# Groups 2 to 7 of layer one's first matrix as seven products of half blocks, with block sums taken from the decode and weight places from a list

## The chip, the cores and the metric

The kernel runs on one core of a Trainium2 chip. The metric is the device time of one execution in microseconds, from runs on the chip. The engines are TensorE (PE; its weight loads are PEld), VectorE (DVE), ScalarE (ACT), GpSimd (POOL) and SyncE (SP), whose queue issues most of the DMA transfers.

## What is computed

An attention with a local window and block summaries, and behind it two layers of two matrices each. x has 1536 tokens of 512 features.

```python
def _moe_ref(x, w_in, w_out):            # layer one: w_in 512x2048, w_out 2048x512
    h = x @ w_in
    g = h * (1.0 / (1.0 + np.exp(-1.702 * h)))
    return (g @ w_out).astype(np.float32)

def _moe2_ref(x, w_gate, w_val, w_out):  # layer two: 512x1536 twice, 1536x512
    gate = 1.0 / (1.0 + np.exp(-(x @ w_gate)))
    val = x @ w_val
    return (gate * val @ w_out).astype(np.float32)

def reference(**kwargs):
    attn_out = _attn_ref(q, k, v)        # 2 batches, 8 heads, 768 tokens, 64 features
    x = attn_out.transpose(0, 2, 1, 3).reshape(1536, 512)
    return _moe2_ref(_moe_ref(x, w_in, w_out), w_gate, w_val, w_out2)
```

## The kernel before

Each factor of a product is held as a high and a low part (H and L), each of a type that TensorE takes in one pass, and a product is three matmuls: low times high, high times low, high times high. Tokens go in three blocks of 512 (`TB`), the 512 features in four chunks of 128 (`KC`), split into `LO` and `HI`. The hidden features go in groups of 256, two halves of 128 each: eight groups in layer one (`n1`), six in layer two (`n2`). A weight comes from memory as 64-bit words into a `raw` buffer (two of them, `fetch`, line 157) and is decoded on DVE and ACT (`decode`, line 91) into a high and a low tile. `load` (line 168) is a generator that stands between other work; `pull` (line 446) takes its next step and `need` (line 451) takes steps until a weight is there.

The weight tiles, 128x1024 each, lie in three rings: `w_a` with 8 places, `w_b` with 4 and `w_c` with 2 (lines 85 and 747). In layer two `w_a` holds the first two matrices, `w_b` the block sums and `w_c` the last matrix.

Layer one works in steps of a group and a token block (line 133). `first` (line 368) makes two projections of 12 matmuls into two PSUM banks (`ps_h`), the sigmoid on ACT, and in `gate_by` (line 358) the product on DVE, the high part on ACT and the low part on POOL. `second` (line 395) makes four steps of 6 matmuls into the banks `ps_o`, and DVE adds each to `acc`. Four (group, block) steps, groups 0 and 1 for blocks 0 and 1, run between the units of the attention (`EARLY`, `filler`); the others follow in a plain loop (line 758) in which `second` of a step runs behind `first` of the next one. There `ps_o` has six banks.

Layer two takes blocks 0 and 1 together. `token_sums` (line 239) makes four combinations of their halves, `combine` (line 200) makes four combinations of the quarters of a weight, for which it first adds high and low part again (line 205), and `pair` (line 262) makes seven products per matrix of 6 matmuls each (`product`, line 117) where the plain form has eight. ACT copies product 1 into a second PSUM bank, onto which products 6, 7 and 4 add, and DVE adds held products to others (`total`, line 289). `single` (line 323) does block 2 in the plain way. In layer two the products take the six banks and `second` the two (line 778), and the steps of `second` stand between products.

Of the program, SP's order is written out by hand; the other engines' orders are worked out at build time from the order of the text and an estimate of each instruction's time, so that an instruction that is ready can be put ahead of an earlier one that isn't.

Of the kernel before, what the change touches and what calls it, by code (L numbers as in the profile page):

```python
# [28 lines left out]
def attention_moe_moe2_kernel(ctx: ExitStack, tc: tile.TileContext, ins: dict, out: bass.AP):  # L29
# [54 lines left out]
    w_slots, sg_slots, gh_slots, gl_slots = (Slots(t) for t in ("w", "sg", "gh", "gl"))  # L84
    w_a = pool([w_slots], 8, "w_a")
    pool([gh_slots, gl_slots], GF, "g_a")
    pool([sg_slots], 2, "sg_a")
    acc_a = ctx.enter_context(tc.tile_pool(name="acc_a", bufs=1))
    ps_h = ctx.enter_context(tc.tile_pool(name="ps_h", bufs=2, space=PSUM))

    def decode(raw, hi_out, lo_out):

        n = raw.shape[1] // 2
# [9 lines left out]
        ts(out=b, in0=tail, scalar1=29, scalar2=None, op0=ALU.logical_shift_right)  # L105
        yield
# [3 lines left out]
        nc.scalar.copy(hi_out, af)  # L110
        yield
        nc.vector.tensor_tensor(out=lo_out, in0=af, in1=hi_out, op=ALU.subtract)
# [19 lines left out]
    groups = [(1, g) for g in range(n1)] + [(2, g) for g in range(n2)]  # L132
    steps = [(1, g, blk) for blk in range(NTB) for g in range(2)]
    steps += [(1, g, blk) for g in range(2, n1 - 2) for blk in range(NTB)]
    steps += [(1, g, blk) for g in (n1 - 2, n1 - 1) for blk in range(2)] + [(1, g, 2) for g in (n1 - 2, n1 - 1)]
# [11 lines left out]
    pieces, weights, raws, ready = [], {}, [], {}  # L147
# [20 lines left out]
    def load(slots, layer, g, i):  # L168
        raw, shape = raws.pop(0)
        hi, lo = (slots.tile(list(shape), F32R, name=f"w{layer}_{g}_{i}{x}") for x in "HL")  # L170
        parts = decode(raw, hi.rearrange("p a n -> p (a n)"), lo.rearrange("p a n -> p (a n)"))
        for step, _ in enumerate(parts):
            if step == 1 and (layer, g) != (1, 0):
                fetch()
            yield
        return hi, lo

    def load_group(layer, g):
        tiles = weights[layer, g] = []
        ready[layer, g] = 0  # L180
        for i in range(len(mats[layer])):
            tiles += yield from load(w_slots, layer, g, i)
            ready[layer, g] += 1
            yield

    class Ring:


        def __init__(self, pool):
            self.pool = pool  # L190

        def tile(self, shape, dtype, name):
            return self.pool.tile(shape, dtype, tag="w", name=name)

# [5 lines left out]
    def combine(g, i):  # L200

        hi, lo = weights[2, g, i]
        flat = "p a n -> p (a n)"
        w, s = (wtmp.tile([P, KC, GF * P], F32, tag=t, name=f"{n}{g}_{i}") for t, n in (("da", "wf"), ("db", "ws")))
        nc.vector.tensor_tensor(out=w.rearrange(flat), in0=hi.rearrange(flat), in1=lo.rearrange(flat), op=ALU.add)  # L205
        yield
        s = s.rearrange("p a (k f) -> p a k f", f=P)
        for n, a, b, op in (
            (0, block(w, 1, 0), block(w, 1, 1), ALU.add),
            (1, s[:, 0], block(w, 0, 0), ALU.subtract),  # L210
            (2, block(w, 0, 0), block(w, 1, 0), ALU.subtract),
            (3, block(w, 0, 1), s[:, 1], ALU.subtract),
        ):
            nc.vector.tensor_tensor(out=s[:, n], in0=a, in1=b, op=op)  # L214
            if n % 2:
                yield
# [3 lines left out]
        nc.vector.tensor_tensor(out=sl.rearrange(flat), in0=s.rearrange(flat), in1=sh.rearrange(flat), op=ALU.subtract)  # L220
        sums[g, i] = sh, sl
        yield

    sums = {}

    def prepare():
# [219 lines left out]
    def pull(n):  # L446
        for _ in range(n):
            if next(coming, True):
                break
# [401 lines left out]
```

## Time and profile before

| | us |
|---|---|
| median of 3 runs | 630.01 (629.63 to 630.9) |
| the profiled execution | 629.99 |
| its span, first to last instruction | 628.1 |
| mean granted clock of TensorE | 0.997 of full |

The attention, with the early steps of layer one, takes the first 124 us, layer one the time to about 340, layer two the rest. "Busy" counts time in which an engine executes; matmuls overlap on PE, so its busy share alone doesn't say that it has no room. The chain of waits is followed back from the last instruction, at each step to what released it.

### The profile page before, as it was taken

The numbers are of one execution on the slowest core, as the hardware profiler recorded it, in microseconds if no ns is written. First come the engines' busy times: TensorE is split into PE (matmuls) and PEld (weight loads), VectorE is DVE, ScalarE is ACT, GpSimd is POOL, SyncE is SP. The second block draws the span as 40 slices with busy tenths as digits, with TensorE's granted clock in tenths as the row PEclk, the third lists the DMA queues.
The fourth block names the chain that finished last, engine by engine and source line by source line (L and its number), as shares of the span: only waits on it lengthen the run. The fifth ranks groups of instructions, "written<-read, shape, count | busy, mean of one in ns | idle before, by whom it ended". The sixth has DMA issues, their size and how long they took to land.

```text
span 628.1 us, 8342 instructions
## 1 busy us (share of the span) xinstructions
PE 613.1 (98%) x3162; PEld 499.9 (80%) x3162; DVE 430.8 (69%) x628; ACT 282.5 (45%) x560; POOL 194.8 (31%) x164
## 2 busy tenths in 40 slices
PE   7898999999999999999999999999999999999997
PEld 4676787778888888888888887888887888888886
DVE  6699666488976665565379995279499479496524
ACT  4688657546443334232246645444344244333310
POOL 6797676233132313132222030120031120130210
PEclk9899999999999999999999999999999999999999
DMA  9997752044521222100001304012113012100004
GB/s 311 347 328 254 242 126 64 2 134 141 176 86 67 68 67 68 67 2 1 0 13 61 129 0 135 0 68 78 57 67 118 17 67 74 61 1 0 2 33 168
DMA packets 25160, 58.08 MB, mean 92 GB/s; under 512 B 1568, under 2 KB 1824, under 8 KB 25120
## 3 DMA queue, kind: packets, MB, share of 16 engines
q1 hardware_dynamic: 24400, 56.24, 27.6%
q10 hardware_dynamic: 720, 1.31, 0.6%
q8 instruction: 25, 0.41, 0.3%
q14 instruction: 15, 0.12, 0.1%
HBM read 53.08 MB, written 3.15 MB: 90 GB/s over the span
## 4 chain that ended last, share of the span: by engine, by line
PE 86%; DVE 9%; ACT 2%; issue 1%; DMA 1%; SPq 0%; DVEq 0%; ACTq 0%
PE ps_o L349 35%; PE ps_h L349 20%; PE ps_v L124 8%; PE ps_y L124 7%; PE ps_x L124 5%; PE ps_h L124 4%; PE ps_s L559 3%; PE ps_x L611 2%; PE ps_p L592 1%; DVE wf L205 1%; DVE ws L214 1%; DMA vt<-in_vt 1%; ACT e L572 1%; DVE nm L564 1%; DVE sg L364 1%
## 5 line engine op out<-in xcount | busy, mean ns | idle before, releaser
L366 POOL TENSOR_TENSOR gl<-sg,gh 128x512 fp32r<-128x512 f32 x84 | 119.5, 1424 | 393.7 <-ACT gh L365 372.0
L429 DVE TENSOR_TENSOR acc<-ps_o,acc 128x512 f32<-128x512 f32 x143 | 97.2, 686 | 56.9 <-PE ps_o L349 56.8
L365 ACT CAST gh<-sg 128x512 fp32r<-128x512 f32 x84 | 52.0, 620 | 89.8 <-DVE sg L364 79.6
L349 PE MATMUL ps_o<-gh,w_1L 128*128 128x512 f32 x192 | 74.5, 395 | 1.6 <-ACT gh L365 1.5
L349 PE MATMUL ps_h<-xH,w_0L 128*128 128x512 f32 x192 | 75.2, 396 | 0.5 <-DVE acc L429 0.5
L349 PE MATMUL ps_o<-gl,w_1H 128*128 128x512 f32 x192 | 75.4, 393 | 0.0
L349 PE MATMUL ps_h<-xL,w_0H 128*128 128x512 f32 x192 | 75.0, 391 | 0.0
L349 PE MATMUL ps_o<-gh,w_1H 128*128 128x512 f32 x192 | 74.8, 390 | 0.0
L349 PE MATMUL ps_h<-xH,w_0H 128*128 128x512 f32 x192 | 74.8, 390 | 0.0
L364 DVE TENSOR_TENSOR sg<-ps_h,sg 128x512 f32<-128x512 f32 x48 | 32.9, 687 | 44.1 <-ACT sg L373 43.8
L349 PE MATMUL ps_o<-w_2H,gl 128*128 128x512 f32 (+1 forms) x146 | 56.2, 388 | 1.0 <-ACT acc L425 0.6
L349 PE MATMUL ps_o<-w_2H,gh 128*128 128x512 f32 (+1 forms) x146 | 56.4, 386 | 0.0
L349 PE MATMUL ps_o<-w_2L,gh 128*128 128x512 f32 (+1 forms) x146 | 56.4, 386 | 0.0
L373 ACT ACTIVATE sg<-ps_h 128x512 f32<-128x512 f32 x48 | 28.3, 595 | 61.2 <-PE ps_h L349 61.2
L107 DVE SCALAR_TENSOR_TENSOR da<-da,db 128x1024 uint32<-128x1024 uint32 x34 | 43.9, 1290 | 14.4 <-ACT da L103 14.0
L103 ACT ACTIVATE da<-da 128x1024 f32<-128x1024 f32 x34 | 36.1, 1061 | 30.6 <-DVE da L102 28.6
L349 PEld LDWEIGHTS ps_o<-gh,w_1L 128*128 128x128 f32 x192 | 35.9, 188 | 9.3 <-ACT gh L365 2.0
L349 PEld LDWEIGHTS ps_h<-xH,w_0L 128*128 128x128 f32 x192 | 36.0, 188 | 8.2 <-DVE acc L429 0.9
L349 PEld LDWEIGHTS ps_h<-xH,w_0H 128*128 128x128 f32 x192 | 36.0, 188 | 7.6
L349 PEld LDWEIGHTS ps_o<-gh,w_1H 128*128 128x128 f32 x192 | 36.1, 188 | 7.3
L349 PEld LDWEIGHTS ps_o<-gl,w_1H 128*128 128x128 f32 x192 | 36.1, 188 | 7.3 <-POOL gl L366 0.2
L349 PEld LDWEIGHTS ps_h<-xL,w_0H 128*128 128x128 f32 x192 | 36.0, 188 | 7.4
(162 smaller groups left out, 1244.5 us busy)
## 6 DMA issues: line engine op xcount, KB each, us to landing
raw<-in_moe_w_out SPq DMA_DIRECT2D x13, 1024.0 KB, 4.9
raw<-in_moe_w_in SPq DMA_DIRECT2D x8, 1024.0 KB, 7.3
raw<-in_moe_w_gate SPq DMA_DIRECT2D x6, 1024.0 KB, 5.1
raw<-in_moe_w_val SPq DMA_DIRECT2D x6, 1024.0 KB, 5.1
q<-in_q SPq DMA_DIRECT2D x20, 256.0 KB, 7.5
vwin<-in_v SPq DMA_DIRECT2D x6, 768.0 KB, 8.1
k<-in_k SPq DMA_DIRECT2D x8, 400.0 KB, 6.5
out<-acc SPq DMA_DIRECT2D x11, 256.0 KB, 2.0
```

Source lines behind the costliest of these rows:

```text
L103: nc.scalar.activation(af, af, AF.Prelu, scale=REBIAS, alpha=-2.0 ** 32)
L107: nc.vector.scalar_tensor_tensor(out=a, in0=a, scalar=3, in1=b, op0=ALU.logical_shift_left, op1=ALU.bitwise_or)
L124: nc.tensor.matmul(ps, lhsT=a[x][:, kk, :], rhs=b[y][:, kk, :], start=start and i == 0, stop=i == n - 1, skip_group_check=True,)
L205: nc.vector.tensor_tensor(out=w.rearrange(flat), in0=hi.rearrange(flat), in1=lo.rearrange(flat), op=ALU.add)
L349: nc.tensor.matmul(ps, lhsT=a, rhs=b, start=i == 0, stop=i == n - 1)
L364: nc.vector.tensor_tensor(out=sg, in0=val, in1=sg, op=ALU.mult)
L365: nc.scalar.copy(gh, sg)
L366: nc.gpsimd.tensor_tensor(out=gl, in0=sg, in1=gh, op=ALU.subtract)
L373: nc.scalar.activation(sg, ps, AF.Sigmoid, scale=1.702 if layer == 1 else 1.0)
L429: nc.vector.tensor_tensor(out=a[:, m, :], in0=ps, in1=a[:, m, :], op=ALU.add)
L559: nc.tensor.matmul(ps[:, j, :], lhsT=t[:, j, :], rhs=kt[:, j, :], start=False, stop=j == G - 1)
L611: nc.tensor.matmul(ps[64 * e:64 * e + 64, j, :], lhsT=x[:, h * D:(h + 1) * D], rhs=y[:, j, 64 * e:64 * e + 64], start=n == 0, stop=n == le ...
```

## The change

Layer one's groups 2 to 7 now take `pair` and `single`, as layer two does. For them the combinations of blocks 0 and 1 of the attention's output are made by `input_sums` in twelve steps, eight of them between the last units of the attention. A weight's block sums are made in `load`, straight from the decoded value, with no addition of high and low part, in layer two as well; `combine` is gone. Layer one's order of products is 1, 5, 2, 6, 3, 7, 4, and steps of `second` stand behind products as the lists in the last hunk say: in a pair those of block 2 of the group before, beside the single products those of blocks 1 and 0 of the same group, two behind each. From group 2 on `second` has two PSUM banks and the products six. Group 6's block 2 is done after group 7's pair, so that blocks 0 and 1 end before block 2. Weight places are no longer rings: `w_free` is a list of 14 places (8 and 6), `take` takes the one that was freed first and `drop` gives a weight's places back. A decode whose places are not free waits in the text, not on the engine.

```diff
+    def places(n, name):
+        p = ctx.enter_context(tc.tile_pool(name=name, bufs=1, reuse_waits="tile"))
+        w_free.extend((p, f"{name}{i}") for i in range(n))
+    def take(shape, name, key):
+        p, tag = w_free.pop(0)
+        w_held.setdefault(key, []).append((p, tag))
+        return p.tile(shape, F32R, tag=tag, name=name)
+    def drop(*key):
+        w_free.extend(w_held.pop(key))
+    places(8, "w_a")
...
+    def load(layer, g, i, early):
...
+        if (layer, g, i) == (1, 1, 1):
+            scratch.append(wraw.tile([P, KC, TB], F32, tag="raw", name="scratch"))
+        elif not early:
+            fetch()
         yield
...
+        while len(w_free) < 2:
+            yield
+        hi, lo = (take(list(shape), f"w{layer}_{g}_{i}{x}", (layer, g, i)) for x in "HL")
...
+        if layer == 1 and (g < 2 or i == 1) or layer == 2 and i == 2:
+            return
+        w = af.rearrange("p (a n) -> p a n", n=shape[2])
+        s = wtmp.tile([P, 4, KC // 2, P], F32, tag="db", name=f"ws{layer}_{g}_{i}")
+        for n, x, y, op in (
+            (0, block(w, 1, 0), block(w, 1, 1), ALU.add),
+            (1, s[:, 0], block(w, 0, 0), ALU.subtract),
+            (2, block(w, 0, 0), block(w, 1, 0), ALU.subtract),
+            (3, block(w, 0, 1), s[:, 1], ALU.subtract),
+        ):
+            nc.vector.tensor_tensor(out=s[:, n], in0=x, in1=y, op=op)
+            if n == 1:
+                yield
+        while len(w_free) < 2:
+            yield
...
+        nc.scalar.copy(sh.rearrange(flat), s.rearrange(flat))
+        yield
+        nc.vector.tensor_tensor(out=sl.rearrange(flat), in0=s.rearrange(flat), in1=sh.rearrange(flat), op=ALU.subtract)
...
-    def combine(g, i):
...
+    def input_sums():
+        tt = nc.vector.tensor_tensor
+        f1, f3 = scratch[0][:, LO], scratch[0][:, HI]
+        f2 = t_a.tile([P, KC // 2, TB], F32, name="f2")
+        h1, l1, h3, l3 = (t_tile(x) for x in ("1H", "1L", "3H", "3L"))
+        def whole(to, blk, half):
+            tt(out=to, in0=xH[blk][:, half], in1=xL[blk][:, half], op=ALU.add)
+        whole(f1, 0, LO)
+        yield
+        whole(f3, 1, LO)
+        yield
+        tt(out=f1, in0=f3, in1=f1, op=ALU.subtract)
+        yield
+        whole(f2, 1, HI)
+        yield
+        tt(out=f3, in0=f2, in1=f3, op=ALU.subtract)
+        nc.scalar.copy(h3, f3)
+        yield
...
+        tt(out=l2, in0=f2, in1=h2, op=ALU.subtract)
+        fetch()
...
         def out(i, to, x, own=None):
+            if layer == 1:
+                gate = sg_slots.tile([P, TB], F32, "sg")
+                nc.scalar.activation(gate, x, AF.Sigmoid, scale=1.702)
+                gate_by((1, g, *to), x, gate)
+                return
...
-        for n in "1256734":
-            for i in range(2):
+        for n in ("1526374", "1256734")[layer - 1]:
+            for i in range(layer):
...
+            if t >= 4 * HP + LD:
+                next(folding)
...
+        places(6, "w_b")
...
+        def run(main, rest=iter(()), after=()):
+            for n, _ in enumerate(main):
                 pull(1)
                 next(folding, None)
+                for _ in range(after.count(n)):
+                    next(rest, None)
+            for _ in rest:
+                pull(1)
+                next(folding, None)
...
+        for g in range(2):
+            run(first(1, g, 2))
+            drop(1, g, 0)
+            if g == 0:
+                run(second(1, 0, 2, False))
+                drop(1, 0, 1)
         ps_f, ps_o, o_tag = ps_o, ps_h, "h"
+        top = n1 - 1
+        for g in range(2, n1):
+            need((1, g, 0), (1, g, 0, "s"))
+            for _ in folding if g == 2 else ():
+                pass
+            if g < top:
+                run(pair(1, g), second(1, g - 1, 2, False), (0, 2, 4, 5))
+                drop(1, g - 1, 1)
+            else:
+                run(pair(1, g), seconds(1, g - 1, 1, 0), range(7))
+            drop(1, g, 0, "s")
+            need((1, g, 1))
+            if g != top - 1:
+                n = min(g, top - 1)
+                run(single(1, n), seconds(1, g, 1, 0), (0, 0, 1, 1, 2, 2, 3, 3))
+                drop(1, n, 0)
+        folding = token_sums()
+        run(single(1, top), second(1, top - 1, 2, False), range(4))
```

## Rows read from the trace of the kernel before

**Rows 1.** The page: engine totals (busy us, share, instructions), and granted clock in 40 slices.

```profile
PE 613.1 (98%) x3162; PEld 499.9 (80%) x3162; DVE 430.8 (69%) x628; ACT 282.5 (45%) x560; POOL 194.8 (31%) x164
...
PEclk9899999999999999999999999999999999999999
```

**Rows 2.** The chain of waits in order of time: start us, us, what.

```profile
64.10 0.69 PE ps_x L611 x16
...
160.62 5.44 PE ps_o L349 x24
...
367.27 2.21 DVE wf L205
...
476.30 2.72 PE ps_x L124 x12
```

**Rows 3.** Busy time by stretches: us, then engines (x instructions), clock, DMA share, GB/s.

```profile
160.00:320.00 160.00, 160.00 (x707) 132.55 (x706) 100.44 (x138) 55.80 (x81) 42.15 (x30) 1.00 0.17 53
400.00:600.00 200.00, 199.72 (x882) 164.96 (x881) 141.97 (x187) 78.46 (x113) 38.34 (x27) 1.00 0.14 48
```

**Rows 4.** What PE waited for, 64 us to the end: us, times, longest.

```profile
PE ps_o L349 <- ACT acc L425: 0.6, 1, 0.6
PE ps_x L611 <- DVE pt L597: 0.6, 1, 0.6
PE ps_h L349 <- DVE acc L429: 0.5, 1, 0.5
PE ps_o L349 <- DVE acc L429: 0.3, 1, 0.3
```

**Rows 5.** Busy time by stretches, the two slices in which PE's count falls.

```profile
360.00:380.00 20.00, 19.58 (x87) 15.89 (x85) 19.76 (x27) 9.74 (x14) 5.46 (x4) 1.00 0.08 18
...
460.00:480.00 20.00, 19.72 (x88) 16.00 (x87) 19.06 (x24) 7.78 (x12) 6.73 (x5) 1.00 0.10 31
```

**Rows 6.** Groups on DVE: line, shapes, count | busy us, mean ns | idle before, releaser.

```profile
L107 DVE SCALAR_TENSOR_TENSOR da<-da,db 128x1024 uint32<-128x1024 uint32 x34 | 43.9, 1290 | 14.4 <-ACT da L103 14.0
...
L112 DVE TENSOR_TENSOR w_0L<-da,w_0H 128x1024 fp32r<-128x1024 f32 x14 | 18.5, 1325 | 1.5 <-ACT w_0H L110 1.5
...
L220 DVE TENSOR_TENSOR sL<-ws,sH 128x1024 fp32r<-128x1024 f32 x12 | 14.6, 1216 | 2.0 <-ACT sH L219 2.0
L214 DVE TENSOR_TENSOR ws<-wf 128x256 f32<-128x256 f32 x24 | 10.5, 479 | 0.2
L205 DVE TENSOR_TENSOR wf<-w_1H,w_1L 128x1024 f32<-128x1024 f32 x6 | 10.5, 1743 | 0.2
...
L205 DVE TENSOR_TENSOR wf<-w_0H,w_0L 128x1024 f32<-128x1024 f32 x6 | 9.2, 1541 | 0.1
L290 DVE TENSOR_TENSOR sg<-ps_y,sg 128x512 f32<-128x512 f32 x12 | 8.2, 687 | 8.7 <-PE ps_y L124 8.7
...
L249 DVE TENSOR_TENSOR acc<-acc,acc 128x1024 f32<-128x1024 f32 x3 | 3.6, 1208 | 0.0
```

**Rows 7.** Groups on POOL and ACT, columns as in rows 6.

```profile
L366 POOL TENSOR_TENSOR gl<-sg,gh 128x512 fp32r<-128x512 f32 x84 | 119.5, 1424 | 393.7 <-ACT gh L365 372.0
...
L373 ACT ACTIVATE sg<-ps_h 128x512 f32<-128x512 f32 x48 | 28.3, 595 | 61.2 <-PE ps_h L349 61.2
...
L219 ACT CAST sH<-ws 128x1024 fp32r<-128x1024 f32 x12 | 12.7, 1055 | 11.6 <-DVE ws L214 8.5 <-PE ps_o L349 2.9 <-PE ps_h L349 0.2
```

**Rows 8.** Busy time by stretches, a slice at the end of the attention.

```profile
100.00:120.00 20.00, 19.98 (x169) 15.65 (x168) 9.97 (x24) 14.41 (x48) 9.54 (x9) 1.00 0.01 1
```

**Rows 9.** The chain of waits where the attention has ended.

```profile
125.76 1.23 DVE w_0L L112
127.64 8.50 PE ps_h L349 x36
```

**Rows 10.** The timeline at the end: start us, us, engine, operation, [idle before, releaser].

```profile
623.26 0.69 DVE L429 TENSOR_TENSOR acc<-ps_o,acc 128x512 f32<-128x512 f32 x1 [0.67 <-PE ps_o L349]
...
624.01 0.19 PEld L349 LDWEIGHTS ps_o<-w_2H,gl 128*128 128x128 f32 x1 [0.28 <-DVE acc L429]
```

More of the change, by code (lines that the diff above doesn't have):

```diff
@@ L131, in attention_moe_moe2_kernel @@
     n2 = w_gate.shape[1] // (GF * P)
[L132 to L135, printed above, removed]
+    steps = [(1, g, blk) for blk in range(2) for g in range(2)]
     ends = {1: n1 - 1, 2: n2 - 1}
@@ L166, in fetch @@
             raws.append((raw, (P, n, m // 2)))
[L168 to L184, printed above, removed]
@@ L224, in attention_moe_moe2_kernel, with t_tile @@
[L224 to L237 removed]
+    def t_tile(name):
+        return (t_b if name[0] == "2" else t_a).tile([P, KC // 2, TB], F32R, tag=f"t{name}", name=f"t{name}")
@@ L260, in attention_moe_moe2_kernel, with pair @@
     tsum = {}
-    def pair(g):
+    def pair(layer, g):
         def sums_of(n, i):
-            return tuple(x[:, n] for x in sums[g, i])
+            return tuple(x[:, n] for x in weights[layer, g, i, "s"])
         def a(i, r, c):
-            return tuple(block(x, r, c) for x in weights[2, g, i])
+            return tuple(block(x, r, c) for x in weights[layer, g, i])
         b11, b21, b22 = ((xH[n][:, h], xL[n][:, h]) for n, h in ((0, LO), (0, HI), (1, HI)))
@@ L321, in pair, with single @@
                 yield
-    def single(g):
+    def single(layer, g):
         for f in range(GF):
             sg = None
-            for i in range(2):
-                wh, wl = weights[2, g, i]
+            for i in range(layer):
+                wh, wl = weights[layer, g, i]
                 ps = ps_f.tile([P, TB], F32, tag="o", name="ps_h" if i == 0 else "ps_v")
@@ L443, in attention_moe_moe2_kernel, with need @@
     EARLY_UNITS = 10
-    coming = (x for n in range(2) for x in load_group(*groups[n]))
+    order = [(1, g, i) for g in range(n1) for i in range(2)] + [(2, 0, 0), (2, 0, 1)]
+    for g in range(n2):
+        order += [(2, h, i) for h, i in ((g + 1, 0), (g, 2), (g + 1, 1)) if h < n2]
+    coming = (x for n, key in enumerate(order) for x in load(*key, n < 2))
     def pull(n):
         for _ in range(n):
-            if next(coming, True):
-                break
-    def need(layer, g, n):
-        while ready.get((layer, g), 0) < n:
-            pull(1)
+            next(coming, None)
+    def need(*keys):
+        for key in keys:
+            tries = 0
+            while key not in weights:
+                pull(1)
+                tries += 1
+                assert tries < 100, (key, w_free, w_held)
     with tc.manual_schedule(engines={mybir.EngineType.SP}), ExitStack() as es:
@@ L798, in attention_moe_moe2_kernel @@
                 pass
-            while (2, g, 2) not in ready:
-                pull(1)
-            rest = (x for blk in range(2) for x in second(2, g, blk, g == ends[2]))
-            for _ in single(g):
+            drop(*prev, prev[0])
+            drop(2, g, 0, "s")
+            drop(2, g, 1, "s")
+            need((2, g, 2))
+            rest = seconds(2, g, 0, 1)
+            for _ in single(2, g):
                 ahead(g + 1)
```

135 lines of the change are left out of this document (55 added, 80 removed).

## The prediction

> **What bounds the kernel now.** I read the page's engine totals and its line of granted clock first. TensorE is busy 98% of the span at full clock (2.4 GHz), DVE 69% [rows 1]. A busy PE isn't yet a bound PE, because its instructions overlap, so next comes the chain of waits in order of time. From 64.10 us to layer two it holds almost only PE pieces, and there the price of a matmul is to be seen: 24 of 128x512 take 5.44 us, and 12 of a seven-product stage of layer two take 2.72 us [rows 2]. Both are 0.2267 us per matmul, from one start to the next.
>
> Then the busy time by stretches: 707 matmuls in layer one from 160 to 320 us, 882 in layer two from 400 to 600, a few of them cut by the edges [rows 3]; 160 / 0.2267 = 706 and 200 / 0.2267 = 882. So PE doesn't pause in layer one, and hardly in layer two. The waits that PE shows from 64 us to the end add up to 2.0 us in four places [rows 4]. In two slices of 20 us its count falls below 90: three short in 360 to 380, two in 460 to 480, both with DVE busy over 19 of 20 us [rows 5]. So from 64 us on the time is the number of PE's instructions, and a matmul that goes is worth 0.2267 us, less what the edit makes PE wait.
>
> **What the change removes.** In groups 2 to 7 the first matrix, for token blocks 0 and 1, is 2 blocks x 2 halves x 12 = 48 matmuls now, and seven products of 6 = 42 after. That is 6 per group, 36 in all: 36 x 0.2267 = **8.16 us**, all in stretches where PE has no pause. Block 2 keeps its 24 and the second matrix its 72, so a group of layer one goes from 144 matmuls (32.64 us) to 138 (31.28 us). The products have the shape that costs 0.2267 us in layer two.
>
> **What it adds, beside PE.** DVE's operations of 128x512 take 0.69 us. Per group of layer one it gets four block sums of 128x256 at 0.48 us = 1.9, one low part at 1.22, two totals at 0.69 = 1.4: 4.5 us [rows 6]. It is busy 100.4 of 160 us in layer one now [rows 3], 20.5 us per group; that becomes 25.0 of 31.28 us, 80%. In layer two the two additions that put high and low part together again go (L205, 1.54 and 1.74 us), 12 in all, 19.7 us; its 142 of 200 us there, 71%, falls by 3.3 us in a group of 204 matmuls (46.2 us), to 64%. The input sums are 12 operations of 128x1024 at 1.21 us (as the token sums, L249) = 14.5 us once [rows 6]. Over the kernel DVE goes from 430.8 by 27 + 14.5 - 19.7 to about 453 us. ACT gets per group a cast of 1.06 and three copies of 0.6 us, and four casts for the inputs [rows 7]: 21 us, on an engine busy 45% [rows 1]. None of them becomes the bound on the mean; what can cost is the moment at which each is needed.
>
> **Those moments.** *Input sums, first eight steps*, at the end of the attention: they stand in DVE's queue among the reductions and copies of the last units. DVE is busy 9.97 of 20 us from 100 to 120 [rows 8], and 8 x 1.21 = 9.7 us just about fit, while PE has early matmuls of layer one to run. The ends are 0 and 9.7; I take 0.5, near the one wait of PE for DVE in that stretch (0.6, ps_x for pt) [rows 4].
>
> *Start of group 2.* PE starts on block 2 at 127.64 and the weight places are free at 125.76 at the latest, where w_0L is written into one [rows 9]. 72 matmuls come before the first pair, and 12 before product 5, the first that needs sums: 84 x 0.2267 = 19.0, with the 1.9 before them 20.9 us. In that time DVE must do four input sums 4.8, the low part of the weights 1.33, the block sums and their low part 3.1, four gate products 2.75, up to four additions to acc 2.75 and, if put ahead, the second matrix' decode of four operations at 1.33 at most, 5.3 [rows 6]: 20.0 us. It fits, barely: 0 here, and what it costs if it doesn't is a rival.
>
> *A load buffer held long.* The scratch tile of the input sums sits in one of two raw buffers, so the load of (1,3,0) goes only when they are done, some 10 us after 125.76. Nothing stands behind it on SP's queue but later weights, and the sums made of it are needed a group (31 us) after the first pair's start near 144: 0.
>
> *Inside a pair.* Product 6 adds onto a bank that ACT fills with product 1 (0.6 us, with a product and a step of the second matrix between): 0. Product 4 writes the bank that DVE's total of product 7 reads. The kernel's last additions show such a turn: DVE starts at 623.26, about 0.2 us after PE could have gone on, takes 0.69, and the next group's first matmul is at 624.01 [rows 10]: 0.95 us. One step of the second matrix, 1.36 us, stands between 7 and 4. It fits if DVE is free; with a decode operation of 1.29 us just begun, 0.95 + 1.29 - 1.36 = 0.88 us is left. At a DVE 80% busy I take 0.15 per pair, 0.9 us in six; the ends are 0 and 5.3.
>
> *The gates of block 1.* The second matrix of a group follows right behind its pair, where it ran a block later before. The gate of product 7 needs total and product on DVE, sigmoid and cast on ACT, the difference on POOL: 0.69 + 0.6 + 0.69 + 0.6 + 1.42 = 4.0 us [rows 6, 7]. PE has a step, product 4 and 24 matmuls of block 2 to put ahead, 8.2 us: 0; without the 24, 1.3 us per group.
>
> *Weight places.* 14 before (8 + 4 + 2), 14 after (8 + 6); in layer one at most 12 are held, the next group's first matrix and sums among them: 0. In layer two half of the sums can now be made during a pair, not all after it, which spreads the work of the slices of rows 5.
>
> *The passage to layer two.* There the chain leaves PE for DVE, with the addition L205 at 2.21 us its dearest piece [rows 2]. The additions that go are dearest there, and (2,0,0) is prepared earlier. Of the 1.2 us that PE loses in the two slices of rows 5 I take 0.8 as regained; the ends are 0 and 2.0, all waits of rows 4.
>
> **The sum.** The profiled run took 629.99 us (628.1 of span, 1.9 around it), 0.02 from the median of 630.01. 629.99 - 8.16 + 0.5 + 0.9 - 0.8 = 622.4; I predict **622.4 us**.
>
> **Rivals.** *More is gained*: no new waits, and all old ones go, 629.99 - 8.16 - 2.0 = 619.8. For it: DVE's relief in layer two. Against it: most of the old waits lie before or at the first pairs, where DVE gets more to do.
>
> *DVE comes late*, at the start or in the pairs. Up to 5.3 us in the pairs; at the start, additions of two SBUF tiles cost 1.21 us at L249 but 1.74 at L205 [rows 6], and at that price (x 1.44) the ten such operations in the list, 10.5 us, grow by 4.6 and outlast their cover by 3.7 us. One half of each, with 0.9 of the first already in the sum: 622.4 + 1.75 + 1.85 = 626.0. The Trainium skill (SBUF — State Buffer, Who interferes with whom) has a rule for that spread: a DVE instruction with both inputs in SBUF contends with a GpSimd instruction that reads SBUF. The 1.21 and 1.74 agree with it; as POOL is busier in the attention than later, it speaks for the dear price in the first eight input sums.
>
> *Slower: two banks for the second matrix.* In layer one its steps had six banks and have two. During the single products of block 2 two steps follow each product, so a bank is wanted again after one step and one product, 2.72 us. The addition that frees it takes 0.2 + 0.69; behind two decode operations of 1.29 us it is 3.47, a wait of 0.75. There are 48 such steps; from 11 of them that wait the gain of 8.16 is gone, and with 20 it is 629.99 - 8.16 + 15 = 636.8. Against it: layer two has the same two banks with DVE 71% busy, and PE has no pause that counts in 200 us [rows 3]; but there one step stands beside each product. The Trainium skill (Perfetto Trace Analysis, Matmuls) wants independent matmul groups to rotate through different PSUM banks, so that one's evacuation overlaps the next's matmuls; it makes this the dangerous part, and layer two's row shows that two banks do for one step at a time.
>
> *No change*: the 36 matmuls go and each group gives its 1.36 us back, 0.88 between 7 and 4 and half a microsecond for a bank: 629 to 631.
>
> **How the numbers follow.** Forecast 0.55, more gained 0.12, DVE late 0.21, no change 0.07, slower 0.05. Within 0.2% (1.26 us, about what a measurement of this kernel tells from no change) lies the no-change case; faster are the first three, 0.88. The range takes in more gained and most of DVE late: 619.6 to 627.0.
>
> **What would show it.** PE's count falls from 3162 to 3126 and layer one stays at 90 matmuls per 20 us. Waits of PE for DVE between 145 and 330 us of about 1 us in total bear out the step I put at 0.9; above 4 it is DVE late; if they are ps_o for acc, it is the two banks. The first matmul of block 2 starts within 0.5 us of 127.64. DVE is at 80% in layer one and 64% in layer two. I am wrong if group 2 starts over 2 us late, or if the chain lies on DVE for more than a few microseconds in layer one.

## The result, and the profile after

The changed kernel takes **638.0 us** (median of 4 runs, 636.54 to 638.32), the kernel before 630.13 in runs on the same chip: a ratio of 1.0119, 95% interval 1.0100 to 1.0139. It is slower; the forecast was 622.4 us, with a range of 619.6 to 627.0.

The page of the kernel after: engine totals, granted clock, and the chain's shares by engine, which answer to [rows 1].

```profile
PE 611.9 (96%) x3126; PEld 494.6 (78%) x3126; DVE 465.2 (73%) x670; ACT 300.8 (47%) x588; POOL 203.8 (32%) x164
...
PEclk9898989999999999999999999999999999999999
...
PE 78%; DVE 12%; ACT 6%; DMA 2%; issue 1%; POOL 0%; SPq 0%; ACTq 0%; DVEq 0%
```

The 36 matmuls are gone, 3162 to 3126, and the kernel takes 8 us more: some 16 us of new losses of PE. The busy time by stretches shows where (us, then busy time of the engines with their instructions, granted clock, DMA share, GB/s). A slice of 20 us at full rate holds 90 matmuls of 512 columns, so each that is missing is 0.2267 us. (20 / 0.2267 is 88; a matmul across an edge counts in both slices, so a sum of such losses is good to about half a microsecond.)

```profile
80.00:100.00 20.00, 17.73 (x132) 14.19 (x131) 17.29 (x32) 11.28 (x47) 16.26 (x18) 0.91 0.49 123
100.00:120.00 20.00, 18.91 (x154) 15.02 (x153) 15.88 (x25) 15.18 (x47) 11.05 (x10) 1.00 0.13 26
...
200.00:220.00 20.00, 20.00 (x90) 16.57 (x89) 8.50 (x13) 6.09 (x10) 3.82 (x4) 1.00 0.00 1
...
300.00:320.00 20.00, 19.31 (x85) 15.69 (x84) 14.73 (x20) 7.91 (x12) 4.92 (x4) 1.00 0.06 11
320.00:340.00 20.00, 16.05 (x64) 11.49 (x63) 19.73 (x27) 8.49 (x11) 8.54 (x5) 1.00 0.25 95
340.00:360.00 20.00, 19.90 (x87) 15.88 (x87) 19.93 (x24) 12.39 (x19) 2.61 (x3) 1.00 0.00 1
...
400.00:600.00 200.00, 200.00 (x884) 165.59 (x884) 126.23 (x168) 79.20 (x116) 37.12 (x25) 1.00 0.14 48
```

Against [rows 8] the slice from 100 to 120 us has 15 PE instructions fewer and 5.9 us more of DVE. From 320 to 340 us 26 of 90 matmuls are missing; over 260 to 360 us it is 40 of 450, 9.1 us. What PE waited for from 64 us on (us, times, longest), against [rows 4]:

```profile
PE ps_o L381 <- DVE acc L461: 5.5, 6, 2.0
PE ps_s L595 <- ACT e L610: 3.2, 2, 2.3
PE ps_h L381 <- DVE sg L396: 1.8, 1, 1.8
PE ps_o L381 <- POOL gl L398: 0.7, 1, 0.7
```

The account, in spans: 628.1 before; -8.16 for the matmuls; **+7.0** up to the first matmul of block 2 (134.68 instead of 127.64, [rows 9]); **+1.8** at 140 us, the wait of ps_h for sg; **+9.1** at the end of layer one; -1.1 for the five matmuls that were missing in [rows 5] and no longer are (a third slice, 380 to 400 us, has 87 in the kernel before as well and 90 after). That gives 636.7; the span is 636.5. Three places are to be explained: A, the attention; B, the start of layer one; C, its end.

In C the chain of waits (start us, us, what) leaves PE for DVE's decode of layer two's first matrices:

```profile
311.49 1.37 PE ps_o L381 x6
...
314.49 2.04 DVE w_0L L137
...
324.62 1.48 DVE ws L150
...
330.76 1.70 DVE da L128
...
332.49 1.74 DVE ws L150 x2
```

DVE's timeline there (start us, us, line, operation, out<-in):

```profile
321.28 0.75 DVE L150 TENSOR_TENSOR ws<-da 128x256 f32<-128x256 f32 x2
321.95 0.42 DVE L150 TENSOR_TENSOR ws<-ws,da 128x256 f32<-128x256 f32 x1
322.28 0.69 DVE L461 TENSOR_TENSOR acc<-ps_o,acc 128x512 f32<-128x512 f32 x1
322.88 1.82 DVE L137 TENSOR_TENSOR w_1L<-da,w_1H 128x1024 fp32r<-128x1024 f32 x1
324.62 1.48 DVE L150 TENSOR_TENSOR ws<-da,ws 128x256 f32<-128x256 f32 x1
326.03 0.68 DVE L461 TENSOR_TENSOR acc<-ps_o,acc 128x512 f32<-128x512 f32 x1
```

From 315.4 to 342.5 us PE runs 90 matmuls of ps_o without a break, fifteen steps of the second matrix; from the first start to the last, 89 intervals take 20.2 us at full rate and took 27.1. Before there were never more than 24 (as the one in [rows 2]). Each step, 1.36 us on PE, needs its addition to acc before its bank is free, and there are two banks. Between two additions stands decode or block-sum work of layer two: here 1.82 + 1.48 us, and the addition that PE needs at about 324.7 starts at 326.03.

### The profile page after: what moved, and what is told of

Same layout as the page of the kernel before. It is cut to its first block, busy times and chain, and to the rows that moved or that the text cites. A ratio compares the mean times of both kernels' runs of the same rounds, so it can differ in the third digit from the quotient of the medians.

```text
span 636.5 us, 8302 instructions
## 1 busy us (share of the span) xinstructions
PE 611.9 (96%) x3126; PEld 494.6 (78%) x3126; DVE 465.2 (73%) x670; ACT 300.8 (47%) x588; POOL 203.8 (32%) x164
## 4 chain that ended last, share of the span: by engine, by line
PE 78%; DVE 12%; ACT 6%; DMA 2%; issue 1%; POOL 0%; SPq 0%; ACTq 0%; DVEq 0%
PE ps_o L381 31%; PE ps_v L172 12%; PE ps_y L172 11%; PE ps_h L172 10%; PE ps_x L172 7%; DVE acc L461 2%; ACT e L610 2%; PE ps_h L381 2%; PE ps_s L597 2%; DVE w_0L L137 1%; DVE da L128 1%; DMA vt<-in_vt 1%; PE ps_x L649 1%; DVE ws L150 1%; DVE nm L602 1%
## 5 line engine op out<-in xcount | busy, mean ns | idle before, releaser
L398 POOL TENSOR_TENSOR gl<-sg,gh 128x512 fp32r<-128x512 f32 x84 | 126.1, 1509 | 386.7 <-ACT gh L397 308.7
L381 PE MATMUL ps_o<-gh,w_1L 128*128 128x512 f32 x192 | 77.0, 408 | 7.0 <-DVE acc L461 5.5
L128 DVE SCALAR_TENSOR_TENSOR da<-da,db 128x1024 uint32<-128x1024 uint32 x34 | 44.1, 1297 | 11.7 <-ACT da L120 11.1
L610 ACT ACTIVATE e<-ps_s,nm 128x128 f32<-128x128 f32 x96 | 34.2, 375 | 13.9 <-DVE nm L602 11.2
L586 POOL TENSOR_SCALAR kx<-k 128x384 f32<-128x384 f32 x24 | 31.4, 1310 | 16.4 <-DMA k<-in_k 11.8
L624 POOL TENSOR_TENSOR e<-e,rr 128x512 f32<-128x512 f32 x24 | 28.2, 1183 | 13.3 <-DVE rr L619 11.1
L381 PEld LDWEIGHTS ps_o<-w_2H,gl 128*128 128x128 f32 x146 | 27.4, 188 | 5.9 <-DVE acc L461 0.3
L381 PEld LDWEIGHTS ps_o<-w_2L,gh 128*128 128x128 f32 x146 | 27.4, 188 | 5.6
L381 PEld LDWEIGHTS ps_o<-w_2H,gh 128*128 128x128 f32 x146 | 27.4, 188 | 5.5
L122 DVE TENSOR_SCALAR db<-raw 128x1024 uint32<-128x1024 uint32 x33 | 31.1, 941 | 0.4
L597 PE MATMUL ps_s<-kx,q 128*128 128x128 f32 x192 | 29.8, 309 | 0.9 <-POOL kx L586 0.8
```

The costliest lines, as they stand in the source:

```text
L128: nc.vector.scalar_tensor_tensor(out=a, in0=a, scalar=3, in1=b, op0=ALU.logical_shift_left, op1=ALU.bitwise_or)
L381: nc.tensor.matmul(ps, lhsT=a, rhs=b, start=i == 0, stop=i == n - 1)
L398: nc.gpsimd.tensor_tensor(out=gl, in0=sg, in1=gh, op=ALU.subtract)
L586: nc.gpsimd.tensor_scalar(out=to, in0=x, scalar1=scale, scalar2=None, op0=ALU.mult)
L597: nc.tensor.matmul(ps[:, j, :], lhsT=t[:, j, :], rhs=kt[:, j, :], start=False, stop=j == G - 1)
L610: nc.scalar.activation(e[:, j, :], s[:, j, :], AF.Exp, bias=nm[:, j:j + 1], accum_out=sm[:, j:j + 1])
```

## The experiments

Times are medians; 'before' is 629.5 to 630.1 us in the runs on the same chips. The experiments stand in the order of what they settled. C1 to C4, A1 and A2 are the theories that the expectations name. Lost matmuls are those missing from 90 in slices of 20 us between 260 and 360 us, x 0.2267.

### A: the input sums and the step count of the decode

The chain of waits of the kernel after runs through the input sums (lines 230 to 260) in the attention:

```profile
87.07 1.38 DVE scratch L230
...
90.24 1.28 DVE scratch L236
...
93.87 1.69 DVE t1L L248
```

**Input sums left out.**

```diff
-        whole(f1, 0, LO)
...
+        for n, (blk, half) in {"1": (0, LO), "2": (0, HI), "3": (1, HI), "4": (1, LO)}.items():
+            tsum[n] = xH[blk][:, half], xL[blk][:, half]
```

> Leaves out the twelve DVE operations and four ACT casts of the input sums: the pairs of layer one multiply by the plain halves of the input, so the output is not the reference's; PE's work is the same. The changed kernel starts block 2 of layer one at 134.7 us, 7.0 later than the kernel before. If the input sums' own time on DVE makes that (theory A1), block 2 starts at 128 to 130, the wait of 1.9 us at 140 goes too, and the time falls from 638.0 to 630 to 632. If the earlier place of the decode of (1,2,0) in DVE's order makes it (theory A2), block 2 still starts at 133 to 135 and the time is 636 to 638.

636.6 us. Block 2 starts at 130.80 us, 3.9 earlier, between the two theories, and the wait at 140 us (B) is gone. Yet only 1.4 us reach the end: 51 matmuls are missing at the end of layer one, 11.6 us instead of 9.1. So A costs time, and C takes back what is won ahead of it.

**Input sums later in the text** (the call in the attention's loop removed).

```diff
-            if t >= 4 * HP + LD:
-                next(folding)
```

> All twelve steps of the input sums stand behind the attention in the text, none between its last units. Theory A1: block 2 starts at 128 to 131, but 12 operations of 1.2 to 1.5 us then come into the 19 us before the first pair's fifth product, where group 2 may start up to 5 us late: 632 to 636. Theory A2: block 2 still starts at 133 to 135, and the time is 637 to 641.

637.95 us, block 2 at 134.0 us. The scheduler that orders each engine put the sums into the attention all the same: a place in the text doesn't hold ready work back.

**Only four matrices loaded in the attention.**

```diff
-    coming = (x for n, key in enumerate(order) for x in load(*key, n < 2))
+    coming = (x for n, key in enumerate(order[:4]) for x in load(*key, n < 2))
...
+        coming = (x for key in order[4:] for x in load(*key, False))
```

> In the attention only the first four weights are decoded in the text; (1,2,0) and what follows stand behind it, as in the kernel before. Theory A1: 636 to 638, block 2 starts at 133 to 135. Theory A2: the copy of the block means to vwin leaves SP's queue at 63 instead of 67.2 us, block 2 starts 3 to 4 us earlier, and the time is 633 to 635.

640.33 us, longer than either theory has it, block 2 at 133.9 us: the fifth matrix' decode isn't the cause by itself.

**The step count.** ACT's timelines before and after show what is: `load` now yields four times per matrix in groups 0 and 1, where the kernel before had five steps, so the decode runs ahead and second-matrix steps come earlier. Their copies of acc stood on ACT ahead of the copy of vs, for which the load of vwin, and on SP's queue the load of k behind it, wait. ACT's timeline of the kernel after, where ACT stands idle for ps_o before each copy, and its chain of waits behind vs (line 538 loads vwin):

```profile
63.44 1.07 ACT L457 COPY acc<-ps_o 128x512 f32<-128x512 f32 x2 [2.77 <-PE ps_o L381]
...
66.11 0.58 ACT L457 COPY acc<-ps_o 128x512 f32<-128x512 f32 x1 [1.20 <-PE ps_o L381]
```

```profile
66.59 0.59 ACT vs L569
67.20 0.61 SPq L538
...
67.90 4.11 DMA k<-in_k
```

The next kernel has the fifth step again, nothing of the fifth matrix before the attention's end (the edit of the run before), and the input sums left out:

```diff
         weights[layer, g, i] = hi, lo
         yield
+        if layer == 1 and g < 2:
+            yield
```

> The input sums left out, as in the first run, and the decode pulled as in the kernel before (five steps for each of the first four matrices, nothing of the fifth before the attention's end). In the first run block 2 started at 130.8 us, 3.2 us late. If the step count is what is left of that delay (the four copies of acc ahead of the copy of vs on ACT, and so the loads of vwin and k 4 us late), vs runs near 62.4 us, the load of vwin is issued near 63 us and block 2 starts at 127.6 to 128.2 us. If it is something else in the attention (more decode on DVE, the load buffer), block 2 stays at 130 to 131 us. The end: the loss at the end of layer one grows again as in the first run, if DVE is full there: 633 to 636 us; if that loss stands by itself, 632 us or less.

633.09 us. The copy of vs on ACT in the kernel before, after, and in this one (start us, us):

```profile
62.40 0.59 ACT L531 ACTIVATE vs<-ps_v 32x512 f32<-32x512 f32 x1
```

```profile
66.59 0.58 ACT L569 ACTIVATE vs<-ps_v 32x512 f32<-32x512 f32 x1
```

```profile
61.16 0.59 ACT L538 ACTIVATE vs<-ps_v 32x512 f32<-32x512 f32 x1
```

Block 2 starts at 126.40 us, 1.2 earlier than before the change: with the sums out and the five steps back, A and B are gone. C is 49 matmuls, 11.1 us.

**Five steps with the sums in**, nothing of the fifth matrix before the attention's end, and the sums later in the text:

> The scheduler's order on TensorE as in the changed kernel; only the attention's decode as in the kernel before (five steps for each of the first four matrices, nothing of the fifth before the attention's end, input sums behind the attention in the text). Nothing is left out. By the runs without input sums the step count is worth 4.4 us: block 2 at 129 to 131 us. The run of 90 matmuls at the end of layer one stays, and with it a loss of 8 to 11 us: 633 to 636 us. If the time is under 631 us, the order is not what holds the end of layer one.

637.82 us, over the expected range; block 2 at 133.76. With the sums in, block 2 gains 0.9 us, where 4.4 were expected from the difference without them: the two prices don't add. With vs at 63.93, PE no longer loses its time at 86 us but in one wait of 3.8 us that ends at 105.58, for e (ACT) behind input sums on DVE.

### C: neither the block sums nor the places

**Block sums of layer one left out, their places still filled.**

```diff
-        for n, x, y, op in (
+        for n, x, y, op in () if layer == 1 else (
...
+        if layer == 1:
+            nc.scalar.copy(sh.rearrange(flat), af)
```

> Leaves out the block sums of layer one's first matrix: the four additions and the subtraction of the low part on DVE are gone for groups 2 to 7 (some 3.8 us of DVE per group, 22.6 us in all, by the rows of the changed kernel: 0.655, 0.655, 0.59 and 0.6 us and 1.24 us). Two weight places per group are still taken and filled, by two copies on ACT, and the seven products run on what they hold, so TensorE does the same 3126 matmuls. Theory C2 (DVE is full at the end of layer one): the 8.9 us lost between 260 and 360 us go, the attention stays as it is: 629 to 631 us. Theory C1 (the second matrix has only two banks): the run of 18 steps of the second matrix still waits for its two banks: 636 to 638 us. Theory C3 (the decode stands still for want of weight places, and DVE has its work in bursts): the places are held as before, the bursts stay and only their height falls: 633 to 636 us.

640.95 us, outside all three. Block 2 starts at 138.4 us, 3.8 later than in the kernel after (the edit adds two copies on ACT per matrix; that they make it isn't shown), and at the end of layer one 42 matmuls are missing, 9.5 us. So the block sums' time isn't what makes C, and C2 in that form falls.

**Two more weight places** (`places(8, "w_b")` for `places(6, "w_b")`).

> Two more weight places (16 in place of 14), all else as in the changed kernel. C3: the decode runs one matrix further ahead, DVE's busy share in 200 to 300 us rises and in 320 to 360 us falls under 18 of 20 us; the loss of 8.9 us falls to 4 or less: 632 to 634 us. C2 and C1: nothing, 637 to 639 us.

648.34 us: block 2 at 140.2 us, 58 matmuls missing, 13.1 us, and more waits for POOL's gl (4.8 us). C3 falls, and the scheduler's order is seen to be touchy: more freedom made both the attention and the end worse.

**All sums out, five steps.**

> All sums of layer one left out (input sums and block sums; the seven products run on plain halves and on copies), and the decode is pulled in the attention as in the kernel before: five steps for each of the first four matrices, and nothing of the fifth before the attention's end. The 36 matmuls are still gone. If the sums' time on DVE and the step count are all that stood against the 8.16 us, block 2 starts at 127.6 us as before and the time is 620 to 622 us. If the pairs themselves cost (banks, gates in pairs, the order of the second matrix), it stays above 625 us.

632.2 us. Block 2 is back at 127.6 us, and with no sum of layer one on any engine C is still there. Its busy time by stretches, DVE the third engine:

```profile
300.00:320.00 20.00, 16.94 (x72) 12.95 (x71) 17.07 (x24) 9.21 (x13) 6.30 (x4) 1.00 0.16 52
320.00:340.00 20.00, 16.14 (x67) 11.74 (x66) 18.75 (x23) 9.68 (x15) 7.91 (x5) 1.00 0.17 54
```

It has the run of 90 matmuls too (305.4 to 333.3 us).

### C: the run on two banks

**Six banks for the second matrix in layer one, two for the single products.**

```diff
-                ps = ps_f.tile([P, TB], F32, tag="o", name="ps_h" if i == 0 else "ps_v")
+                p, tag = (ps_h, "h") if layer == 1 else (ps_f, "o")
+                ps = p.tile([P, TB], F32, tag=tag, name="ps_h" if i == 0 else "ps_v")
...
-        ps_f, ps_o, o_tag = ps_o, ps_h, "h"
+        ps_f = ps_o
```

> In layer one, from group 2 on, the second matrix shares the pool of six PSUM banks with the pairs, and the single products take the pool of two; layer two is as it was. The changed kernel loses 8.9 us of PE from 255 to 345 us, 5.5 of it in waits of ps_o for the addition to acc. If two banks make that (theory C1), the loss there falls to 1 to 2 us and the time to 630 to 632. If DVE is simply full there (19.7 of 20 us from 320 to 340) and the banks only show it (theory C2), PE waits for layer two's sums a little later instead, and the time stays at 636 to 638.

637.49 us, but from 260 to 340 us not one matmul is missing, and a run of 56 from 330.1 to 342.6 us is at full rate. Instead 20 are missing from 160 to 220 us and 19 from 340 to 380 us: ps_o waits 2.3 us for POOL's gl in the first stretch and 2.2 in the second. The single products now stand on two banks; that this makes the waits isn't shown. By its total it speaks for C2, read by slices for the banks.

**The same banks with all sums out and five steps.**

> As the run with all sums of layer one left out and five decode steps per matrix (632.2 us, of which 10 us are lost between 260 and 340 us and 1.8 us behind it), and in layer one from group 2 on the second matrix shares the six banks with the pairs, while the single products take the two. If the two banks make that loss (with a step of the second matrix needing its addition on DVE done within one step of 1.36 us, while a decode operation of 0.7 to 1.8 us stands between any two additions): the loss goes and the time is 620 to 623 us. If the order makes it, whatever the banks: 628 us or more.

**623.81 us**, ratio 0.9906 (0.9891 to 0.9921), 8.4 us under the same kernel on two banks, 0.8 over the range given for the banks and far from the one for the order:

```profile
300.00:320.00 20.00, 20.00 (x90) 16.57 (x89) 19.96 (x30) 9.90 (x15) 8.12 (x7) 1.00 0.15 53
320.00:340.00 20.00, 20.00 (x90) 16.54 (x89) 19.82 (x25) 12.44 (x18) 4.24 (x3) 1.00 0.00 1
340.00:360.00 20.00, 20.00 (x90) 16.57 (x89) 19.31 (x26) 11.30 (x17) 2.80 (x2) 1.00 0.30 106
```

DVE is full for 60 us, fuller than above, and PE misses nothing: with six banks it runs ahead of the additions and DVE catches up later. A full DVE is not enough to lose the time; the two banks are needed too.

**TensorE in the order of the text**, behind the attention:

```diff
-    with tc.manual_schedule(engines={mybir.EngineType.SP}):
+    with tc.manual_schedule(engines={mybir.EngineType.SP, mybir.EngineType.PE}):
```

> Behind the attention TensorE runs its matmuls in the order in which the kernel's text gives them, instead of the order that the scheduler made; nothing else is changed and nothing is left out. In the scheduler's order every kernel with the change so far had a run of 90 matmuls of the second matrix without a break at the end of layer one (315.4 to 342.5 us, where they need 20.4 us at full rate and took 27.1), while the kernel before never had more than 24; in the text the longest such run is 12 to 24. Theory C4 (the order: the products of the first matrix are brought forward and 15 steps of the second, each with an addition on DVE, are left over for the end): the loss of 8.9 us between 260 and 360 us falls to 3 or less and nothing comes in its place: 630 to 633 us. Theory C2 (DVE has not enough time in layer one, whatever the order): the loss only spreads over 140 to 360 us: 636 to 639 us. The attention isn't touched: block 2 starts at 134 to 135 us in both.

680.47 us, far outside both. The text puts each step right behind the gates that it needs, in layer two as well; PE's dearest wait in that trace from 130 to 640 us:

```profile
PE ps_o L381 <- POOL gl L398: 28.2, 15, 3.1
```

It didn't tell C4 from C2. (Not every kernel before it had a run of just 90: with six banks it was 56, with 16 places 96.) The same order with five steps, and that with six banks, lose the same way (681.05 and 682.93 us):

> The text order of the run before in this list, and the attention's decode as in the kernel before: five steps for each of the first four matrices, nothing of the fifth matrix before the attention's end, and the input sums behind the attention in the text. Nothing is left out. If the step count is worth the 4.4 us that the runs without input sums show for it (block 2 at 130.8 and 126.4 us) and adds to the order's gain: block 2 at 129 to 131 us and 626 to 629 us in all, under the kernel before. If the two don't add (what is won in the attention is lost behind it, as in the first run): 630 us or more.

> As the run before in this list, and in layer one from group 2 on the second matrix shares the six banks with the pairs, while the single products take the two. In the text order the second matrix has two steps behind one another at most, so two banks should do (C1 off): within 1 us of the run before. If the bank count matters even so: 2 us or more faster.

**An order by hand for groups 2 to 7 alone**, block 2's steps behind later products:

```diff
+        with tc.manual_schedule(engines={mybir.EngineType.SP, mybir.EngineType.PE}):
...
-                run(pair(1, g), second(1, g - 1, 2, False), (0, 2, 4, 5))
+                    run(pair(1, g), second(1, g - 1, 2, False), (3, 4, 5, 6))
```

> Nothing left out. In layer one, groups 2 to 7, TensorE's order is that of the text, with the four steps of the second matrix for block 2 put behind the products 4 to 7 of the pair instead of 1, 3, 5 and 6; the attention, groups 0 and 1 and layer two are ordered by the scheduler as before. No run of the second matrix is longer than 12 matmuls there. C4 (the order): the loss between 260 and 360 us falls from 8.9 us to 2 or less, what the order costs elsewhere is under 3 us: 630 to 634 us. C2 (DVE lacks time in layer one, whatever the order): the loss spreads over 160 to 360 us, 636 to 640 us.

638.78 us. The total lies in the range of C2, but its mechanism, a loss spread over 160 to 360 us, doesn't show; the places tell:

```profile
140.00:160.00 20.00, 15.63 (x66) 12.31 (x66) 15.07 (x18) 11.86 (x18) 5.67 (x3) 0.97 0.32 105
160.00:180.00 20.00, 19.18 (x77) 14.74 (x76) 19.66 (x25) 10.50 (x16) 8.68 (x5) 0.94 0.32 106
...
320.00:340.00 20.00, 19.80 (x88) 16.03 (x87) 10.62 (x17) 7.84 (x13) 5.13 (x4) 1.00 0.00 0
```

On the same two banks, with all sums in, two matmuls are missing from 260 to 360 us instead of 40. What that gains is paid round the first pair, where a fixed order can't go round a late product (ps_x waits 2.6 us for ps_y on ACT): 37 matmuls are missing from 140 to 180 us, 11 in the kernel after, and five more from 180 to 200. From there to 360 us two are missing, where C2 wanted the loss.

**Alternating banks**, every other step on one of the six, five steps, nothing left out:

```diff
+            pp, tg = (ps_f, "o") if layer == 1 and g > 1 and m % 2 else (ps_o, o_tag)
```

> Nothing left out. The attention's decode in five steps per matrix, nothing of the fifth matrix before the attention's end (by itself 637.82 us, as the changed kernel). In layer one from group 2 on every second step of the second matrix takes one of the six banks instead of one of the two, so a run of such steps has four banks or more before it must wait for an addition. If the banks make the loss at the end of layer one: 8.5 us fall to 4 or less, 632 to 634 us, with gates waiting in the first pair of layer two as in the run with the six banks. If the order makes it, 637 us or more.

632.64 us, 5.2 under the same kernel without it (637.82). No matmul is missing from 180 to 380 us. Its longest run of ps_o behind 200 us is 21, so the new banks changed the order as well: this run alone doesn't separate the two. The runs with six banks (runs of 56 and 36, nothing lost there) and by hand (two banks, short runs, nothing lost) do: it takes both, a long run and two banks. No run varies the bank count at a fixed order; the nearest are the kernel after's other long run, 42 on two banks from 271.96 to 282.51 us, 1.3 us over full rate, and the 56 on six banks at full rate.

### A again: the sums held back by their data

**One column of block 2's last low half copied into the first sum's place**, so that the sums that write that place can't run before it is there:

```diff
+        nc.vector.tensor_copy(f1[:, 0, 0:1], xL[2][:, KC - 1, TB - 1:TB])
         whole(f1, 0, LO)
```

> As the kernel with alternating banks and five decode steps (632.64 us), with one copy of one column of block 2's low half into the first sum's place ahead of the input sums, so that none of them but the first of two whole halves can run before the attention's last low half is there. Nothing is left out. If the place in the attention is the price (the sums stand between the softmax steps of the last units on DVE): block 2 starts at 126.4 to 128 us instead of 133.5, and group 2, which needs the sums some 25 us later, loses 1 to 4 us on them: 627 to 630 us. If their DVE time is the price wherever it lies: block 2 starts early and group 2 waits as long: 631 to 633 us.

**626.75 us**, ratio 0.9961 (0.9947 to 0.9974): faster than both kernels. Its busy time by stretches and its waits:

```profile
80.00:100.00 20.00, 20.00 (x170) 16.19 (x169) 13.83 (x30) 11.21 (x44) 14.41 (x16) 1.00 0.62 152
...
160.00:180.00 20.00, 16.72 (x72) 13.55 (x73) 19.96 (x25) 9.95 (x15) 8.03 (x6) 1.00 0.25 89
...
320.00:340.00 20.00, 20.00 (x90) 16.57 (x89) 18.52 (x25) 10.27 (x16) 4.99 (x2) 1.00 0.16 53
```

```profile
PE ps_o L384 <- DVE acc L465: 1.8, 1, 1.8
PE ps_o L384 <- ACT gh L400: 1.6, 1, 1.6
PE ps_h L384 <- DVE acc L465: 1.2, 1, 1.2
PE ps_h L384 <- DVE sg L399: 1.1, 1, 1.1
```

Block 2 starts at 128.09 us, 5.4 earlier, and 5.9 us reach the end; two of the twelve sums still run in the attention (84 and 94 us), the others between 125 and 152. So it was mostly the place, not the time on DVE: with five steps and no sums block 2 starts at 126.40, 1.7 earlier still. From 160 to 180 us, where DVE is at 19.96 of 20 us, 18 matmuls (4.1 us) are missing. That isn't shown to be the sums' doing, for the same kernel with its sums in the attention misses 17 there:

```profile
160.00:180.00 20.00, 18.23 (x73) 14.31 (x71) 19.14 (x25) 10.70 (x18) 7.81 (x5) 0.91 0.31 106
```

**The same, with group 2 by full products again**, so that the sums are due a group later:

> As the run before in this list, and group 2 is computed as in the kernel before, by full products for all three blocks, so that its block sums fall away (3.8 us of DVE), its six matmuls come back (6 x 0.2267 = 1.36 us) and the input sums are needed only by group 3, some 30 us later. Nothing is left out. If the sums cost by their place only: block 2 at 126.4 to 128 us, nothing lost for them behind it, 625.5 to 628.5 us, under the kernel before. If the time comes back elsewhere (DVE behind the attention, gates of full products on two banks): 630 us or more.

631.51 us. Block 2 starts at 128.4, but 25 matmuls are missing from 140 to 160 us and the clock there is granted at 0.88 on average: PE waits for gates (sg on DVE 3.7 us, gl on POOL 1.9). The case of 630 or more came true, by the gates that it named; that the two banks of the full products make these waits isn't shown.

## Why the prediction was wrong, point by point

Two steps failed. The attention was charged 0.5 us, for the input sums' time on DVE, and cost 7.0; and the second matrix' two banks, at nothing in the sum, cost 9.1 at the end of layer one. The prediction's own signs say so: block 2 began 7.0 us late, where 0.5 was allowed, and PE's waits for DVE between 145 and 330 us were ps_o for acc, 3.6 us, the sign named for the two banks.

- **36 matmuls, -8.16 us: right as a count.** 3126 are left. With all sums out, five steps and six banks the kernel takes 623.81 us, 5.9 under the kernel before in runs on the same chip: no run shows more of the 8.16. The shares of DVE were right too, 127.5 of 160 us from 160 to 320 us, 80%, and 63% from 400 to 600; its total, 465.2 us, is 12 over the forecast.
- **Input sums, 0.5 taken of 0 to 9.7: the value chosen was wrong.** It was put near a wait of a time when DVE had half of its slice free [rows 8], on the ground that the sums stand among the last units. The scheduler started them at 74 us, among reductions and gates that PE's next units wait for, and they lasted 1.21 to 2.06 us. Left out, they free 3.9 us of block 2's start; held back by their data, 5.4 (with five steps). The dear price that the SBUF rule spoke for was real, 1.5 us on the mean for the twelve, but the place was the larger part.
- **The decode's step count was not in the sum at all.** The text said what the fetches do and not that the decode itself advances by a step per call, four per matrix instead of five. It is the other part of A: without sums 4.4 us, together with the fifth matrix' later decode, which was always changed with it.
- **Start of group 2, 0: nearly right for the wrong place.** No wait for the sums is seen at the first pair; the 1.8 us of B fall 6 us after block 2's start, where a gate's sg stands on DVE behind the next matrix' decode.
- **Inside the pairs, +0.9: next to nothing was lost there.** From 160 to 260 us one of 450 matmuls is missing, and behind that PE's waits of 0.5 us and more are all of ps_o. The turn from product 7 to 4 costs nothing that shows.
- **The two banks, a rival at 0.05 and nothing in the sum: the mechanism was right and its place wrong.** It was priced beside the single products, two steps at a time, from the text's lists. The scheduler brought products forward and left fifteen steps in a row for the end of layer one, where layer two's decode is on DVE too: 9.1 us, by itself more than the 8.16 won. That the rival's 636.8 us lies near the measured 638.0 is luck: it is made of 20 waits of 0.75 us beside single products, and A's 7.0 us are not in it. The argument against it, that layer two has two banks and no pause [rows 3], held only for an order that never shows such a run. The Trainium skill (Perfetto Trace Analysis, Matmuls) has independent matmul groups rotate through different PSUM banks; the runs agree, two banks losing 10.2 us from 260 to 360 us where six lose none, and DVE busier.
- **Passage to layer two, -0.8: right in kind, too small.** 1.1 us for the five matmuls of [rows 5]. The text read two short slices where there are three; with the three matmuls of 380 to 400 us it is up to 1.8.
- **Range and chances.** All terms of the sum were costed by PE's order in the text, which the scheduler didn't keep. None of the rivals had A and C at once, and slower was at 0.05.

Open: why the scheduler brings the products forward (the runs show only that bank counts, places and steps each change its order), how A divides between sums and step count when both are in, as they don't add, and what makes the loss from 160 to 180 us in the fastest whole kernel.

## What to carry to other kernels

Where a scheduler orders the engines, cost a change by the order that it writes: look for the longest run of one kind of step, and compare its time per step (here 1.36 us) with what the evacuating engine does between two of them, times the banks. Work without a deadline that becomes ready early is put ahead of work that others wait for; a data dependence holds it back where its place in the text doesn't. And a generator's count of steps is part of the change: removing one moves everything that is pulled beside it.

## What the runs showed of the hardware

DVE's operations on SBUF tiles alone took one length where POOL was idle and up to several times that where POOL ran beside them: of the kernel after's 72 block sums of 128x256, none of the 52 without POOL was over 0.43 us, and with POOL busy throughout they reached 1.52. With an operand in PSUM nothing changed: all 143 additions to acc, whatever POOL did, took 0.65 to 0.69 us. POOL is stretched as well: gl takes 1.30 us alone. From DVE's timeline of the kernel with the sums held back, and from POOL's:

```profile
140.00 2.31 DVE L137 TENSOR_TENSOR w_1L<-da,w_1H 128x1024 fp32r<-128x1024 f32 x1
```

```profile
135.71 3.83 POOL L401 TENSOR_TENSOR gl<-sg,gh 128x512 fp32r<-128x512 f32 x1 [14.24 <-ACT gh L400]
```

That is what the Trainium skill (SBUF — State Buffer, Who interferes with whom) lets expect of two inputs in SBUF against a GpSimd instruction that reads SBUF; how much of it there would be in this kernel only the trace could say. And a pause of PE can cost twice. The kernel after in stretches of 2 us, columns as above:

```profile
86.00:88.00 2.00, 0.47 (x5) 0.38 (x4) 2.00 (x4) 0.82 (x5) 1.67 (x2) 1.00 0.34 41
...
90.00:92.00 2.00, 2.00 (x9) 1.62 (x8) 2.00 (x4) 0.66 (x2) 1.91 (x2) 0.57 0.00 0
92.00:94.00 2.00, 2.00 (x7) 1.56 (x6) 2.00 (x6) 2.00 (x9) 0.56 (x1) 0.58 0.00 0
```

PE is idle for most of 86 to 88 us, and from 90 to 94, busy throughout, it has a granted clock of 0.57 and 0.58 of its 2.4 GHz, near the lower level of 1.2. Part of A's 7.0 us is that. Not every pause is followed by it: the wait of ps_o at the end of layer one that lasts 2.0 us lies in the slice from 320 to 340 us, whose granted clock is 1.00.
